# Hedgehog values: the low half taken on GpSimd from an fp32 copy instead of on VectorE from PSUM

## Chip, cores and metric

The kernel runs on one core of a Trainium2 chip. The metric is the device time of one execution in microseconds (us); less is better. The engines are named as in the profile: PE (TensorE, matmuls), DVE (VectorE), ACT (ScalarE), POOL (GpSimd, called Pool below) and SP (SyncE, which issues DMAs here). The kernel's own tiles, queues and buffers are named as in its code.

## What is computed

Four attention layers follow each other on a sequence of 2048 tokens with 512 features, each with a residual connection and a layer norm in front: softmax attention (A), Hedgehog linear attention (B), A and B again, with the same weights in both rounds. There are 32 heads of 16 features. The B layer is the one that matters here:

```python
def _B_ref(x, wqkv, w_phi, wo):
    qkv = ...                                  # x @ wqkv, split into q, k, v of 32 heads x 16
    pq = jnp.einsum("bhsd,hdf->bhsf", q, w_phi)
    pk = jnp.einsum("bhsd,hdf->bhsf", k, w_phi)
    phi_q = jnp.concatenate([_softmax(pq, axis=-1), _softmax(-pq, axis=-1)], axis=-1)
    phi_k = jnp.concatenate([_softmax(pk, axis=-1), _softmax(-pk, axis=-1)], axis=-1)
    kv = jnp.einsum("bhsf,bhsd->bhfd", phi_k, v)
    z  = jnp.einsum("bhsf->bhf", phi_k)
    num = jnp.einsum("bhqf,bhfd->bhqd", phi_q, kv)
    den = jnp.einsum("bhqf,bhf->bhq", phi_q, z)[..., None] + 1e-6
    o = num / den
    return o.transpose(...).reshape(B, S, D) @ wo

x = x + _A_ref(_layernorm(x), A_wqkv, A_wo)
x = x + _B_ref(_layernorm(x), B_wqkv, B_w_phi, B_wo)
x = x + _A_ref(_layernorm(x), A_wqkv, A_wo)
x = x + _B_ref(_layernorm(x), B_wqkv, B_w_phi, B_wo)
```

Matmuls that need more than fp16 are done with two fp16 halves: a value is rounded to fp16 (the high half), the rest that this leaves out is kept in a second fp16 (the low half), and three products (high by high, low by high, high by low) are summed. In the code these are the three `PASSES`. The values `v` of the B layer are split in this way.

## The kernel before

The two A layers take most of the time: `LayerA.attention` goes over 8 groups of heads, 4 blocks of queries and 16 tiles of keys, with scores, exp and the product with the values (lines 878 to 892). The change is in the B layers, in `LayerB.feed`, which is called four times per layer, each time for 512 tokens, and goes over four tiles of 128 tokens. I number these sixteen tiles of a layer as steps 0 to 15 (`tt` in the code); step 15 is `last` and has an order of its own.

In one step, PE projects the tile to `pk`, `pq` and `pbv` (12 matmuls each, line 1065). Each of the three is one PSUM bank of the pool `psS`, which has three buffers; one of them is held by the accumulator `kvp` for the whole layer, so that `pk`, `pq` and `pbv` take turns on two, and each waits until the one before the last has been read. Between `pq` and `pbv`, PE transposes the query features of the step before (`turn`, line 1175, the tile `pqt`), which ScalarE copies to `qT` (line 1176). After `pbv`, PE adds the key features of the step before times their values into `kvp` (`gather`, line 1182, from `fk` and `vt`). In steps 0 to 3 and 5 to 8, `between` adds work that the A layer left behind: a last output projection with its residual (`po`, `xt`, lines 586 and 574), after steps 1 and 3 the statistics of a layer norm (lines 390 to 424, the inverse root with three Newton rounds as small Pool operations), and after steps 5 to 8 the transposition of the normalised tokens into `xnTa` (lines 447, 457 on ScalarE, 460 on VectorE).

`expo` (lines 1124 to 1129) makes `f` out of `pk` or `pq`: VectorE takes maximum and minimum of each head and the two differences, ScalarE the exp. `share` (line 1144) divides by the sums: VectorE adds up (`su`, line 1135), inverts (1136) and for the keys scales by `KS` (1138), Pool multiplies `f` by it. `halves` splits the key features into `fk`: the high half on ScalarE (line 1150), the low one on Pool (1151).

The values `vt` are a tile of two fp16 halves, each with 32 rows of 16 values and a seventeenth column that Pool sets to one and to zero by memset at the beginning of a step (lines 1069 and 1070). The high half is copied from PSUM by ScalarE with a factor of 2^-8 (line 1097), the low half is computed from PSUM by VectorE (`low`, line 1092).

The order on PE, VectorE, ScalarE and Pool is that of the program here, as the feeding stage stands under `manual_schedule`: every engine takes its instructions in the order in which the code issues them, and an instruction that waits holds up all behind it on its engine. In the order of the code, a step's second half is: exp for keys, exp for queries, high half of `vt`, share of the keys, `low`, share of the queries, halves of the keys.

Of the kernel before, what the change touches and what calls it, by code (L numbers as in the profile page):

```python
# [9 lines left out]
F32 = mybir.dt.float32  # L10
# [3 lines left out]
AF = mybir.ActivationFunctionType  # L14
ALU = mybir.AluOpType
AX = mybir.AxisListType

P = 128
S = 2048
D = 512  # L20
H = 32
DH = 16
# [28 lines left out]
def mha_hedgehog_stack(ctx, tc, x_in, a_wqkv, a_wo, b_wqkv, b_wphi, b_wo, out, shmin=SHMIN):  # L51
    nc = tc.nc
# [7 lines left out]
    np_ = pool("np", bufs=2)  # L60
# [5 lines left out]
    def big(shape, dt, name):  # L66
        return bigp.tile(shape, dt, tag="big", name=name)
# [307 lines left out]
    class Norm:  # L375
# [83 lines left out]
        def low(self, t, n, ps):  # L459
            nc.vector.tensor_tensor(self.part(1, t, n), ps.rearrange("p u (c x) -> p c u x", c=NC4), self.part(0, t, n), ALU.subtract)  # L460
# [156 lines left out]
    class LayerA:  # L617
# [179 lines left out]
        def feed(self, lns, work):  # L797

            for j, (a, b, c) in enumerate(work):
                ln = lns[j]  # L800
                self.xnT.append(ln.xnT)
                ln.turn01()
                a()
                ln.turn23()
                b()
                c()
                if j == 2:
                    self.head_norms(0)
                self.head(j)
                if j == 2:  # L810
                    self.next_w = self.octet_w(1)
                    self.load_head()
                if 0 < j < NJ - 1:
                    self.head_values(j - 1)
            self.feed_end()
# [220 lines left out]
    class LayerB:  # L1036
# [15 lines left out]
        def feed(self, j, xnT, between=lambda t: None):  # L1052

            if self.kvp is None:
                self.kvp = psS.tile([P, 2, 512], F32, tag="S", name="kvp")
            qT = [big([P, 4, 512], F32, f"qT{j}_{i}") for i in range(2)]
            self.qT.append(qT)
            for t in range(4):
                tt = 4 * j + t

                def project(dst, w, passes=(0, 1, 2)):
                    for i in passes:
                        a, b = PASSES[i]
                        for c in range(NC4):
                            nc.tensor.matmul(dst, xnT[:, a, c, t * P:(t + 1) * P], w(b, c),  # L1065
                                             start=(i == 0 and c == 0), stop=(i == 2 and c == NC4 - 1))

                vt = np_.tile([P, 2, H, 17], F16, tag="yn", name="vt", bufs=5)
                nc.gpsimd.memset(vt[:, 0, :, 16:17], 1.0)
                nc.gpsimd.memset(vt[:, 1, :, 16:17], 0.0)  # L1070
                bank = lambda name: psS.tile([P, 2, 512], F32, tag="S", name=name)[:, 0, :]
                last = tt == NT - 1
                pk = bank("pk")
                project(pk, lambda b, c: self.wqk[:, 1, b, c, :])
                if last:
                    f_k = self.expo(pk)
                    self.kvb = np_.tile([P, 8, 32], F32, tag="yn", name="kvb", bufs=5)
                    nc.gpsimd.memset(self.kvb, 0.0)
                else:
                    pq = bank("pq")  # L1080
                    project(pq, lambda b, c: self.wqk[:, 0, b, c, :])
                if self.lateq is not None and tt < NT - 2:
                    self.turn(*self.lateq)
                pv_ = bank("pbv")
                project(pv_, lambda b, c: self.wv[b][:, c, :])
                if self.latek is not None:
                    self.gather(*self.latek)
                if last:
                    pq = bank("pq")
                    project(pq, lambda b, c: self.wqk[:, 0, b, c, :], (0, 1))  # L1090
                pvh = pv_.rearrange("p (h d) -> p h d", d=DH)
                low = lambda: nc.vector.scalar_tensor_tensor(
                    vt[:, 1, :, 0:16], pvh, 2.0 ** -8, vt[:, 0, :, 0:16], op0=ALU.mult, op1=ALU.subtract)
                if not last:
                    f_k = self.expo(pk)
                    f_q = self.expo(pq)
                nc.scalar.activation(vt[:, 0, :, 0:16], pvh, AF.Copy, scale=2.0 ** -8)
                if last:
                    fk = self.share_split(f_k, low)
                    self.turn(*self.todo)  # L1100
                    self.gather(tt, fk, vt)
                    project(pq, lambda b, c: self.wqk[:, 0, b, c, :], (2,))
                    self.blocks()
                    self.todo = [self.lateq, (tt, self.expo(pq), qT)]
                    for q in self.todo:
                        self.share(q[1], 1.0)
                    return
                self.share(f_k, KS)
                low()
                if tt == NT - 2:  # L1110
                    self.todo = self.lateq
                    self.latek = (tt, self.halves(f_k), vt)
                else:
                    self.share(f_q, 1.0)
                    self.latek = (tt, self.halves(f_k), vt)
                self.lateq = (tt, f_q, qT)
                between(tt)
# [290 lines left out]
```

## Time and profile before

| | us |
|---|---|
| runs: median (lowest to highest) of 3 | 2544.79 (2544.01 to 2545.54) |
| the profiled execution: its own time | 2544.9 |
| the profiled execution: span, first to last instruction | 2543.1 |
| VectorE busy in the span | 970.2 |
| ScalarE busy in the span | 2177.4 |
| Pool busy in the span | 378.4 |
| low half of `vt` on VectorE (L1092), 32 instructions | 22.0 |
| high half of `vt` on ScalarE (L1097), 32 instructions | 18.6 |
| share of `f` on Pool (L1144), 62 instructions | 119.9 |

In the rows of the profile, `out<-in` names the tile written and the tiles read, `x` a count, and the time in brackets how long the engine sat idle before the instruction and which instruction ended that. A row of the order of time begins with the start and the duration in us. A row of the groups by line has the busy time in us and the mean duration of one instruction in ns behind the bar, then the idle time before them. The rows of stretches give for each engine its busy us and its number of instructions, and then the TensorE clock that was granted. The matmuls of one projection are merged into one row.

### The profile page before, as it was taken

To read this page: it belongs to the slowest core of one execution; us is meant where nothing else is said; L and a number is where in the kernel's file an instruction comes from. 1 tells how busy PE (TensorE), PEld (TensorE's weight loads), DVE (VectorE), ACT (ScalarE), POOL (GpSimd) and SP (SyncE) were. 2 spreads that over 40 slices of the span, in tenths; PEclk is the share of its full clock that TensorE was granted. 3 is DMA by queue.
4 is the path that set the end of the run, shared out by engine and by line. 5 is a ranking of instruction groups with operands and counts; after the bars stand their busy time and mean duration, and the time that the engine had idled before them with its cause. 6 is when DMAs were issued, how large, how long until landed. Compare 5 with 4: busy or idle time off the path is not lost.

```text
span 2543.1 us, 51497 instructions
## 1 busy us (share of the span) xinstructions
PE 2436.6 (96%) x21344; PEld 748.5 (29%) x21344; DVE 970.2 (38%) x1884; ACT 2177.4 (86%) x2437; POOL 378.4 (15%) x521
## 2 busy tenths in 40 slices
PE   6799999999999999999889999999999999998998
PEld 3222222222222222345343222222222222224543
DVE  6212211212133316799871112111111111368897
ACT  5699999999999999644438999999999999994553
POOL 2100000101000000266430000000000000004552
PEclk9899999999999999999899999999999999999999
DMA  3510230033033612100234002202300251110003
GB/s 142 104 44 5 43 47 6 14 48 80 1 78 58 232 51 84 51 17 1 75 97 67 14 6 49 41 1 43 52 17 10 61 141 51 67 67 26 9 18 110
DMA packets 109782, 135.34 MB, mean 53 GB/s; under 512 B 63537, under 2 KB 64801, under 8 KB 107361
## 3 DMA queue, kind: packets, MB, share of 16 engines
q1 hardware_dynamic: 108864, 129.59, 20.6%
q8 instruction: 169, 2.77, 0.5%
q0 software_dynamic: 672, 2.36, 0.2%
q14 instruction: 77, 0.62, 0.1%
HBM read 60.06 MB, written 39.85 MB: 39 GB/s over the span
## 4 chain that ended last, share of the span: by engine, by line
PE 77%; DVE 12%; ACT 5%; issue 3%; POOL 2%; SPq 1%; DMA 0%; ACTq 0%; POOLq 0%; DVEq 0%
PE pv L892 37%; PE s L878 21%; PE pqk L586 5%; PE po L586 4%; ACT p L881 3%; DVE su L1135 2%; PE pbv L1065 1%; PE pk L1065 1%; PE pq L1065 1%; DVE f L1127 1%; POOL f L1144 1%; DVE f L1128 1%; DVE mx L1124 1%; DVE yt L531 1%; DVE su L1136 1%
## 5 line engine op out<-in xcount | busy, mean ns | idle before, releaser
L881 ACT ACTIVATE p<-s 128x1024 f32<-128x1024 f32 x2048 | 1887.9, 1114 | 21.4 <-PE s L878 18.8
L892 PE MATMUL pv<-p,v 128*32 128x512 f32 x8192 | 1092.8, 605 | 2.6 <-DVE yt L504 1.8
L878 PE MATMUL s<-kq 49*128 49x512 f16 x3872 | 605.9, 382 | 20.7 <-DMA kq<-sh 12.3
L878 PEld LDWEIGHTS <-kq 49*128 49x128 f16 x3968 | 136.3, 94 | 637.3 <-issue 625.0
L892 PEld LDWEIGHTS pv<-p,v 128*32 128x32 f32 x8192 | 161.8, 108 | 398.6 <-issue 368.5
L688 POOL TENSOR_TENSOR sq<-stg 128x512 bf16<-128x512 f16 x48 | 70.1, 1460 | 1046.1 <-DVE stg L762 943.4
L504 DVE STREAM_TRANSPOSE yt<-pv 128x512 f32<-128x512 f32 x64 | 45.8, 716 | 451.5 <-PE pv L892 429.4
L761 DVE TENSOR_SCALAR tq<-pqk,c_qk 128x512 f32<-128x512 f32 x48 | 35.9, 749 | 445.0 <-PE pqk L586 427.6
L1144 POOL TENSOR_TENSOR f<-f,su 128x1024 f32<-128x1024 f32 x62 | 119.9, 1933 | 381.0 <-DVE su L1138 351.1
L1065 PEld LDWEIGHTS <-xnTa 128*128 128x128 f16 x1152 | 110.2, 98 | 149.8 <-DVE f L1128 23.6
L586 PEld LDWEIGHTS <-wA 128*32 128x32 f16 (+1 forms) x2496 | 87.1, 98 | 202.2 <-issue 177.8
L574 DVE SCALAR_TENSOR_TENSOR xt<-po,c_oA,xt 128x512 f32<-128x512 f32 x64 | 47.1, 736 | 234.5 <-PE po L586 224.1
L586 PE MATMUL pqk<-xnTb,wA 128*32 128x512 f16 (+1 forms) x1248 | 118.5, 381 | 2.2 <-ACT xnTb L457 2.2
L586 PE MATMUL pqk<-xnT,wA 128*32 128x512 f16 (+1 forms) x1224 | 111.0, 379 | 3.1 <-ACT xnT L457 2.6
L1129 ACT ACTIVATE f<-f,c_pB 128x1024 f32<-128x1024 f32 x64 | 72.6, 1148 | 45.3 <-DVE f L1128 45.2
L1065 PE MATMUL pbv<-wbv,xnTa 128*128 128x512 f16 x384 | 91.4, 389 | 19.0 <-DVE f L1128 19.0
L1150 ACT ACTIVATE fk<-f 128x1024 f16<-128x1024 f32 x30 | 31.7, 1057 | 74.4 <-POOL f L1144 74.4
L586 PE MATMUL po<-woA,ob 128*32 128x512 f16 x1152 | 92.4, 379 | 0.0
L1065 PE MATMUL pk<-wbqk,xnTa 128*128 128x512 f16 x384 | 88.5, 379 | 0.0
L1065 PE MATMUL pq<-wbqk,xnTa 128*128 128x512 f16 x384 | 88.4, 379 | 0.0
L1135 DVE TENSOR_REDUCE su<-f 128x64 f32<-128x1024 f32 x64 | 77.5, 1211 | 9.4 <-ACT f L1129 8.8
L586 PE MATMUL po<-wbo,obB 128*128 128x512 f16 x336 | 75.9, 385 | 0.6 <-POOL obB L524 0.6
(280 smaller groups left out, 1858.8 us busy)
## 6 DMA issues: line engine op xcount, KB each, us to landing
kq<-stg SPq DMA_DIRECT2D x168, 128.0 KB
xd<-xt SPq DMA_DIRECT2D x40, 512.0 KB
xt<-xd SPq DMA_DIRECT2D x40, 512.0 KB
v<-vyt SPq DMA_DIRECT2D x384, 16.0 KB
oD<-osp SPq DMA_DIRECT2D x24, 256.0 KB
ob<-oD SPq DMA_DIRECT2D x8, 768.0 KB
xt<-in_A_x_dram SPq DMA_DIRECT2D x8, 512.0 KB
wbqk<-dBqk SPq DMA_DIRECT2D x2, 2048.0 KB
```

Source lines behind the costliest of these rows:

```text
L504: nc.vector.transpose(yt.rearrange("p a b -> p (a b)"), ps)
L574: nc.vector.scalar_tensor_tensor(xt[:, u, :], ps, co, xt[:, u, :], op0=ALU.mult, op1=ALU.add)
L586: nc.tensor.matmul(ps[r, :], w[:, r], x, start=(n == 0), stop=(n == of - 1), skip_group_check=cols)
L688: nc.gpsimd.tensor_tensor(sq, hi, hi, ALU.mult)
L761: nc.vector.tensor_scalar(tq, ps, cqk, CLAMP, op0=ALU.mult, op1=ALU.min)
L878: nc.tensor.matmul(s[:, u, :], self.side(g, half, r, 0, kt * P, P), self.side(g, half, r, 1, j * 512, 512), start=True, stop=True)
L881: nc.scalar.activation(pt, s, AF.Exp, scale=0.25 / (QS * QS))
L892: nc.tensor.matmul(acc[32 * hh:32 * hh + 32, :], self.oct[o]["v"][:, r:r + 32], pt[:, hh % 2, :], start=(kt == 0), stop=(kt == NT - 1), sk ...
L1065: nc.tensor.matmul(dst, xnT[:, a, c, t * P:(t + 1) * P], w(b, c), start=(i == 0 and c == 0), stop=(i == 2 and c == NC4 - 1))
L1129: nc.scalar.activation(f, f, AF.Exp, scale=con["pB"])
L1135: nc.vector.tensor_reduce(su, f[:, r, :], AX.X, ALU.add)
L1144: nc.gpsimd.tensor_tensor(f3, f3, self.part_sums(f3, slice(0, 64), factor), ALU.mult)
```

## The change

In steps 0 to 14, ScalarE copies `pbv` from PSUM to a new fp32 tile `vf` with the factor of 2^-8, then `vf` to the high half of `vt`; the low half is `vf` minus the high half, on Pool, in the code ahead of the share of the keys. VectorE's `low` is no longer called in these steps. In step 15 everything stays as it was. `vf` takes its buffers from the pool tag `yt`, which has three and is otherwise used in the A layers. Code above line 1097 keeps its line numbers; behind the changed lines they are three higher.

```diff
                 if not last:
                     f_k = self.expo(pk)
                     f_q = self.expo(pq)
-                nc.scalar.activation(vt[:, 0, :, 0:16], pvh, AF.Copy, scale=2.0 ** -8)
                 if last:
+                    nc.scalar.activation(vt[:, 0, :, 0:16], pvh, AF.Copy, scale=2.0 ** -8)
                     fk = self.share_split(f_k, low)
...
                     return
+                vf = np_.tile([P, H, DH], F32, tag="yt", name="vf", bufs=3)
+                nc.scalar.activation(vf, pvh, AF.Copy, scale=2.0 ** -8)
+                nc.scalar.activation(vt[:, 0, :, 0:16], vf, AF.Copy)
+                nc.gpsimd.tensor_tensor(vt[:, 1, :, 0:16], vf, vt[:, 0, :, 0:16], ALU.subtract)
                 self.share(f_k, KS)
-                low()
                 if tt == NT - 2:
```

## The prediction

> **What bounds the kernel now.** I read the page first, then busy time by stretch, then the order of time in the two kinds of step that fill the stretches, and last the groups by line for prices.
>
> ```profile
> PE 2436.6 (96%) x21344; PEld 748.5 (29%) x21344; DVE 970.2 (38%) x1884; ACT 2177.4 (86%) x2437; POOL 378.4 (15%) x521
> ...
> DVE  6212211212133316799871112111111111368897
> ```
>
> Over the span PE is busy 96% and VectorE 38%, but the slices show VectorE at 6 to 9 tenths in two places after the start: where the Hedgehog layers are fed. The change touches only these. The profiled execution took 2544.9 us around a span of 2543.1, and the median of the runs is 2544.79, so the same sum serves for both.
>
> ```profile
> 1047.30:1105.40 58.10, 51.56 (x359) 25.47 (x358) 54.76 (x88) 23.53 (x30) 32.86 (x50) 0.97 0.08 28
> 1105.40:1159.10 53.70, 49.70 (x358) 27.41 (x356) 47.43 (x75) 27.71 (x37) 31.34 (x25) 1.00 0.03 11
> 1159.10:1204.00 44.90, 44.84 (x326) 23.89 (x325) 43.38 (x69) 22.79 (x28) 29.65 (x25) 1.00 0.01 1
> ```
>
> These are the first Hedgehog layer's sixteen token tiles ("steps" 0 to 15), in three stretches (columns: length, then busy PE, weight loads, VectorE, ScalarE, Pool, each with its instructions, and PE's clock); the second layer repeats them. Steps 0 to 4: VectorE is busy 54.76 of 58.10. Steps 5 to 8: neither PE nor VectorE is full. Steps 9 to 13: PE is busy 44.84 of 44.90, so it is PE's stretch. Pool has room on average everywhere, and the average is misleading, as the next rows show. Step 7, the middle kind:
>
> ```profile
> 1132.80 1.15 ACT L1129 ACTIVATE f<-f,c_pB 128x1024 f32<-128x1024 f32 x1 [1.24 <-DVE f L1128]
> ...
> 1133.86 0.58 ACT L1097 ACTIVATE vt<-pbv 128x512 f16<-128x512 f32 x1
> ...
> 1134.52 0.20 DVE L1138 TENSOR_SCALAR su<-su 128x64 f32<-128x64 f32 x1
> 1134.63 0.69 DVE L1092 SCALAR_TENSOR_TENSOR vt<-pbv,vt 128x512 f16<-128x512 f32 x1
> 1134.86 1.93 POOL L1144 TENSOR_TENSOR f<-f,su 128x1024 f32<-128x1024 f32 x1 [4.44 <-DVE su L1138]
> ...
> 1136.83 1.06 ACT L1150 ACTIVATE fk<-f 128x1024 f16<-128x1024 f32 x1 [2.39 <-POOL f L1144]
> ...
> 1137.20 1.93 POOL L1144 TENSOR_TENSOR f<-f,su 128x1024 f32<-128x1024 f32 x1 [0.40 <-DVE su L1136]
> 1137.79 0.58 ACT L457 ACTIVATE xnTa<-pst 128x512 f16<-128x512 f32 x1
> 1138.40 0.69 DVE L460 TENSOR_TENSOR xnTa<-pst,xnTa 128x512 f16<-128x512 f32 x1 [1.38 <-ACT xnTa L457]
> ...
> 1145.97 1.93 POOL L1144 TENSOR_TENSOR f<-f,su 128x1024 f32<-128x1024 f32 x1 [4.43 <-DVE su L1138]
> ```
>
> Pool waits 4.44 us for the small scaling of `su` (L1138), then does the share of `f_k`; ScalarE's `fk` copy waits 2.39 for that; the `xnTa` copy is queued behind it on ScalarE; and VectorE's L460 waits 1.38 for that copy, with the whole next step behind it in VectorE's queue. So the start of the share of `f_k` sets the period, 1145.97 - 1134.86 = 11.11 us. VectorE's low half (L1092) lies beside the share, not in this chain.
>
> ```profile
> 1180.22 1.04 PE L1175 MATMUL pqt<-ident,f 128*128 128x128 f32 x8
> ...
> 1180.86 1.09 ACT L1176 ACTIVATE qT<-pqt 128x512 f32<-128x512 f32 x2 [2.03 <-PE pqt L1175]
> ...
> 1181.83 2.26 ACT L1129 ACTIVATE f<-f,c_pB 128x1024 f32<-128x1024 f32 x2
> ...
> 1184.00 0.58 ACT L1097 ACTIVATE vt<-pbv 128x512 f16<-128x512 f32 x1
> ...
> 1184.85 0.20 DVE L1138 TENSOR_SCALAR su<-su 128x64 f32<-128x64 f32 x1
> ...
> 1185.19 1.94 POOL L1144 TENSOR_TENSOR f<-f,su 128x1024 f32<-128x1024 f32 x1 [2.70 <-DVE su L1138]
> ...
> 1187.53 1.94 POOL L1144 TENSOR_TENSOR f<-f,su 128x1024 f32<-128x1024 f32 x1 [0.40 <-DVE su L1136]
> ...
> 1189.61 1.04 PE L1175 MATMUL pqt<-ident,f 128*128 128x128 f32 x8
> ```
>
> A step of PE's stretch: from one turn of `f_q` to the next 9.39 us (1189.61 - 1180.22). The share of `f_q` ends at 1189.47, 0.14 before the turn that needs it: PE binds, but the loop turn, ScalarE, Pool, turn is just behind.
>
> **The change, part by part.** In 30 steps (15 per layer; step 15 keeps the old way) one VectorE instruction goes, ScalarE gets a second copy, and Pool gets a subtraction that stands *ahead of* the share of `f_k` in Pool's queue. The built order shows it there, behind the memsets; PE's and SyncE's instructions keep their order, and no DMA is added or moved.
>
> ```profile
> L688 POOL TENSOR_TENSOR sq<-stg 128x512 bf16<-128x512 f16 x48 | 70.1, 1460 | 1046.1 <-DVE stg L762 943.4 <-DVE rec L506 102.7
> ...
> L1151 POOL TENSOR_TENSOR fk<-f,fk 128x1024 f16<-128x1024 f32 x30 | 63.9, 2131 | 2.3 <-ACT fk L1150 2.3
> ...
> L524 POOL TENSOR_TENSOR obB<-yb,obB 128x512 f16<-128x512 f32 x32 | 38.3, 1197 | 70.4 <-ACT obB L523 69.0 <-PE pn L1208 1.4
> ...
> L1092 DVE SCALAR_TENSOR_TENSOR vt<-pbv,vt 128x512 f16<-128x512 f32 x32 | 22.0, 686 | 0.0
> ...
> L523 ACT ACTIVATE obB<-yb 128x512 f16<-128x512 f32 x32 | 20.1, 628 | 40.7 <-DVE yb L519 40.5
> ...
> L188 POOL TENSOR_TENSOR wA_s<-wsc,wA_s 128x512 f16<-128x512 f32 x6 | 6.9, 1160 | 1.2 <-ACT wA_s L182 1.1
> ```
> ```profile
> L182 ACT ACTIVATE wA_s<-awk,sA_sc 128x512 f16<-128x512 f32 x3 | 2.1, 708 | 0.0
> ...
> L683 ACT ACTIVATE v<-pv__456 128x512 f32<-128x512 f32 x1 | 0.6, 597 | 3.1 <-PE pv__456 L679 3.1
> ```
>
> Removed: L1092, 0.686 us, of which 0.60 is engine time (the next VectorE instruction starts 0.60 after it in every full stretch). Where VectorE is full this is a gain of at most 0.60 per step; in steps 5 to 8 it only lengthens VectorE's wait for L460.
>
> Added on ScalarE: PSUM to fp32, for which L683 is the same form: 0.59 (597 ns), in the place of the old 0.58. Then fp32 to fp16 within SBUF: L523, 0.63. It reads what the copy before it wrote, so it waits for that one's end; I take 0.03. Bounds for this copy: 0.58 (L1097) and 0.71 (L182).
>
> Added on Pool: L188 is the same subtraction of 512 fp16 from fp32, 1.16; L524 has 1.20; the nearest lower bound is half of the 1024-element L1151, about 1.07, the upper one L688 with 1.46. I take 1.16, since L188 matches also in purpose, and the rows of 16 with a gap cost L1092 and L1097 nothing to be seen. Hand-overs between engines lie between 0.03 and 0.14 in the rows quoted; I take 0.06 into Pool, and 0.04 overlap of Pool instructions in sequence.
>
> [...]
>
> *The wait that is added.* Behind the subtraction on Pool's queue stand the share of `f_k`, that of `f_q`, and the low half of `fk`; for them wait ScalarE's `fk` copy, PE's turn and the gather.
>
> Steps 5 to 8. Before, the share of `f_k` starts 2.06 after the exp of `f_q` does (1134.86 - 1132.80). After: 1.06 to the first copy (1133.86 - 1132.80), +0.59 +0.03 +0.63 +0.06 +1.16 -0.04 = 3.49. Each such step is 1.43 longer. In the first of them another wait counts:
>
> ```profile
> 1105.64 1.93 POOL L1144 TENSOR_TENSOR f<-f,su 128x1024 f32<-128x1024 f32 x1 [0.38 <-DVE su L1136]
> ...
> 1107.63 1.09 PE L1175 MATMUL pqt<-ident,f 128*128 128x128 f32 x8
> ...
> 1109.29 2.19 ACT L1129 ACTIVATE f<-f,c_pB 128x1024 f32<-128x1024 f32 x2
> ...
> 1112.66 1.93 POOL L1144 TENSOR_TENSOR f<-f,su 128x1024 f32<-128x1024 f32 x1 [2.67 <-DVE su L1138]
> ```
>
> The turn in step 5 waits for the share of `f_q` (1107.57 to 1107.63), and both exps come behind its evictions on ScalarE. That share comes 1.43 late, less the 0.40 for which it now waits on its own sums: 1.03. From the exps to the share of `f_k` it is 3.37 before (1112.66 - 1109.29); after, 2.09 for the two exps less overlap, then the same copies and subtraction, 4.52: 1.15 more. So step 5 costs 2.18, and four steps 2.18 + 3 x 1.43 = 6.47.
>
> Steps 9 to 13. Entering, the turn is again 1.03 late. Then the loop closes upon itself: turn to eviction 0.64, to the exps 0.97, exps 2.09, first copy 0.59 + 0.03, second 0.63 + 0.06, subtraction 1.16 - 0.04, shares 1.89 + 1.93, hand-over to PE 0.06: 10.01, against PE's 9.39. Three such periods lie between the turns of steps 9 and 12: 3 x 0.62 = 1.86. Together 2.89.
>
> Step 14 and the end:
>
> ```profile
> 1209.06 0.89 PE L1182 MATMUL kvp<-vt,fk 128*128 128x68 f16 x23 [1.18 <-POOL fk L1151]
> ...
> 1212.77 0.20 PE L1182 MATMUL kvp<-vt,fk 128*128 128x68 f16 x1 [0.22 <-ACT fk L1165]
> ...
> 1213.63 1.20 PE L1182 MATMUL kvp<-vt,fk 128*128 128x68 f16 x23 [0.66 <-DVE fk L1166]
> ```
>
> The gather waits for Pool's low half of `fk`, now 1.43 later within its step; PE's later waits of 0.22 and 0.66 take up 0.88. Cost 0.55.
>
> Steps 0 to 4. Four step ends could each gain 0.60, -2.4. Against it: the turn of step 0 comes late as above, holding up the exps of step 1, and in steps 1 and 3 Pool's small inverse-root operations stand behind its three big ones, now later. I take 0. The lower bound is -2.4; the upper one comes from a collision:
>
> ```profile
> 1068.74 2.13 POOL L1151 TENSOR_TENSOR fk<-f,fk 128x1024 f16<-128x1024 f32 x1
> 1068.90 2.00 DVE L398 TENSOR_SCALAR ly<-lu 128x2 int32<-128x2 int32 x1
> ```
>
> L398, two elements wide, took 2.00 us: it began in Pool's `fk` and ended with it at 1070.90. After the change it arrives while the share of `f_q` still runs. If it gets in at that one's end, it is no later than now; if only after the `fk` that follows, it is 2.1 later, and in step 3 all of VectorE's next step with it: the upper bound is +2.1. [...]
>
> Sum: 0 + 6.47 + 2.89 + 0.55 = 9.9 per layer, 19.8 for two; 2544.9 + 19.8 = 2564.7 us.
>
> **Rivals.** *VectorE's relief decides* (faster). For it: 94% busy in steps 0 to 4, and Pool's average of 33 of 58 us. The gain would be 0.60 in the nine steps 0 to 8, 5.4 per layer: 2534.0. It holds if the share of `f_k` isn't moved, that is if both copies and the subtraction with their hand-overs fit into the 1.0 us (2.06 - 1.06) that `su` takes anyway; by the rows they need 2.43. At about 1.0 us less than that, a subtraction of some 0.2, the sum changes sign (ten of a layer's steps scale with it). Against it: no Pool row of this size is near 0.2. Chance 0.05.
>
> *Pool's share of the time is covered after all*, within 0.2%, which is 5 us and about what a measurement of this kernel can tell from no change: the delay per step would have to be a quarter of mine, as if Pool began with half of the second copy still to come. Nothing shows it. About 2547; chance 0.03.
>
> *Pool is dearer than its rows* (slower still): at 1.46 for the subtraction the sum rises by 10 x 0.30 = 3.0 per layer, and with L398 late by 2.1 it is 15.0, 2574.9. For it: the 2.00 above, and L688's 1.46. Against: L188 is the closer form. Chance 0.22.
>
> That the change doesn't do what it says can be left out, as the built order has the three new instructions in all 30 steps.
>
> **How the numbers follow.** My forecast has 0.70. The range goes from the low bounds (1.07 and 0.58 instead of 1.16 and 0.63: -0.14 in ten steps; steps 0 to 4 at -2.4; 6.1 per layer, 2557.1) to the dear rival with the second copy at 0.71 on top (0.08 in ten steps of two layers, 2576.5): 2556 to 2577. Slower 0.92 (forecast and dear rival), same 0.03, faster 0.05.
>
> **What would show it.** In the profile after: Pool's share of `f_k` released by Pool's own queue, no longer by L1138; its subtraction near 1.16; VectorE waiting about 3.4 us, not 1.38, for `xnTa` in steps 6 to 8 (1.43 and 0.60 more); periods of 12.5 there and of 10.0 in steps 10 to 12, with PE now idle before each turn. Wrong would be: periods of 9.4 there, a subtraction below 0.5, or a share of `f_k` that starts ahead of the subtraction.

## The result, and the profile after

The changed kernel takes 2572.05 us (median of 5 runs, 2571.09 to 2577.38), the one before 2544.79 (5 runs, 2543.59 to 2548.24): a ratio of 1.0111, 95% interval 1.01 to 1.0122. It is 27.3 us slower, where 19.8 were forecast. The execution that was profiled is the slowest of the five: 2577.38 us around a span of 2575.6. Its trace therefore shows some 5 us more than the median, and I come back to where they lie.

The page after, busy time and VectorE's slices:

```profile
PE 2449.3 (95%) x21344; PEld 752.3 (29%) x21344; DVE 962.6 (37%) x1854; ACT 2196.5 (85%) x2467; POOL 409.6 (16%) x551
...
DVE  6211211212133416878861122112121111468787
```

30 instructions have left VectorE, 30 each have come to ScalarE and Pool, and PE, with the same 21344 matmuls, is busy 12.7 us longer. PE's granted clock over the whole span is 0.980, where it was 0.983, and the short stretches below show where it drops. The three new operations, in the groups by line:

```profile
L1111 POOL TENSOR_TENSOR vt<-vf,vt 128x512 f16<-128x512 f32 x30 | 33.6, 1120 | 367.4 <-ACT vt L1110 367.4
L1110 ACT ACTIVATE vt<-vf 128x512 f16<-128x512 f32 x30 | 19.0, 633 | 0.9
L1109 ACT ACTIVATE vf<-pbv 128x512 f32<-128x512 f32 x30 | 17.7, 589 | 3.5 <-PE pbv L1065 3.5
```

1.12, 0.63 and 0.59, against 1.16, 0.63 and 0.59 in the prediction. The first layer's stretches after (columns as in the prediction; cut where steps 5 and 10 begin on VectorE and near the end of step 14, as the prediction's are, so that its second stretch also holds step 9):

```profile
1047.30:1109.90 62.60, 52.96 (x357) 25.58 (x356) 55.31 (x83) 26.49 (x34) 37.07 (x55) 0.95 0.07 26
1109.90:1170.96 61.06, 52.22 (x357) 27.52 (x356) 44.71 (x69) 31.03 (x41) 36.44 (x31) 0.97 0.03 9
1170.96:1218.50 47.54, 45.87 (x328) 23.98 (x326) 41.29 (x63) 25.78 (x33) 34.60 (x29) 1.00 0.01 2
```

In the first one PE's granted clock is 0.95 (0.97 before), in the second 0.97 (1.00 before). Only in the third is it full, and there PE, busy 44.84 of 44.90 before, now has gaps.

Steps 6 and 7 in the order of time, the chain that the prediction followed:

```profile
1131.51 3.82 POOL L1147 TENSOR_TENSOR f<-f,su 128x1024 f32<-128x1024 f32 x2
...
1140.56 1.15 ACT L1132 ACTIVATE f<-f,c_pB 128x1024 f32<-128x1024 f32 x1 [1.25 <-DVE f L1131]
1141.61 0.58 ACT L1109 ACTIVATE vf<-pbv 128x512 f32<-128x512 f32 x1
1142.22 0.63 ACT L1110 ACTIVATE vt<-vf 128x512 f16<-128x512 f32 x1
1142.27 0.20 DVE L1141 TENSOR_SCALAR su<-su 128x64 f32<-128x64 f32 x1
1142.93 1.12 POOL L1111 TENSOR_TENSOR vt<-vf,vt 128x512 f16<-128x512 f32 x1 [5.21 <-ACT vt L1110]
1144.01 3.82 POOL L1147 TENSOR_TENSOR f<-f,su 128x1024 f32<-128x1024 f32 x2
...
1147.55 0.69 DVE L460 TENSOR_TENSOR xnTa<-pst,xnTa 128x512 f16<-128x512 f32 x1 [3.37 <-ACT xnTa L457]
```

The sums `su` are ready at 1142.47, but the share of `f_k` starts at 1144.01, straight behind the subtraction: no instruction is named as its releaser any more, Pool's own queue holds it. The period is 1144.01 - 1131.51 = 12.50 (11.11 before), and VectorE waits 3.37 for `xnTa` (1.38 before). In PE's stretch:

```profile
1184.00 1.09 PE L1178 MATMUL pqt<-ident,f 128*128 128x128 f32 x8 [0.42 <-POOL f L1147]
...
1190.16 3.82 POOL L1147 TENSOR_TENSOR f<-f,su 128x1024 f32<-128x1024 f32 x2
...
1194.04 1.09 PE L1178 MATMUL pqt<-ident,f 128*128 128x128 f32 x8 [0.43 <-POOL f L1147]
```

From turn to turn 10.04 (9.39 before), with PE now idle 0.43 until Pool's shares are done (1190.16 + 3.82 = 1193.98).

What the prediction had not expected lies ahead and behind. Step 3, first before, then after:

```profile
1092.43 1.92 POOL L1144 TENSOR_TENSOR f<-f,su 128x1024 f32<-128x1024 f32 x1
1094.25 0.17 DVE L397 TENSOR_SCALAR lu<-mv 128x2 f32<-128x2 f32 x1
1094.32 2.12 POOL L1151 TENSOR_TENSOR fk<-f,fk 128x1024 f16<-128x1024 f32 x1
1094.52 1.94 DVE L398 TENSOR_SCALAR ly<-lu 128x2 int32<-128x2 int32 x1
1096.38 0.68 DVE L1124 TENSOR_REDUCE mx<-pk 128x32 f32<-128x512 f32 x1
```
```profile
1095.42 1.92 POOL L1147 TENSOR_TENSOR f<-f,su 128x1024 f32<-128x1024 f32 x1
1095.52 3.94 DVE L397 TENSOR_SCALAR lu<-mv 128x2 f32<-128x2 f32 x1
1097.31 2.12 POOL L1154 TENSOR_TENSOR fk<-f,fk 128x1024 f16<-128x1024 f32 x1
1099.57 0.17 DVE L398 TENSOR_SCALAR ly<-lu 128x2 int32<-128x2 int32 x1
1099.64 0.68 DVE L1127 TENSOR_REDUCE mx<-pk 128x32 f32<-128x512 f32 x1
```

Before, L397 came just as the share of `f_q` ended, and L398 alone was caught, in the low half of `fk`. After, L397 comes 0.10 into the share and ends with the low half of `fk` at 1099.43: two elements per partition, 3.94 us, through both Pool instructions. The next step begins 3.26 later than before (1099.64 - 1096.38). This is one of four such places in the trace. In the other three (step 1 of either layer, step 3 of the second) L397 ends with the share of `f_q`, after 1.39 to 1.44 us, and L398 is then held until the low half ends; the last section has such rows.

The end of the layer, one row of before and then the rows after, and PE's clock in two short stretches after (the last columns are the clock, DMA share and GB/s):

```profile
1209.78 1.89 PE L1065 MATMUL pq<-wbqk,xnTa 128*128 128x512 f16 x8
```
```profile
1222.76 0.20 PE L1185 MATMUL kvp<-vt,fk 128*128 128x68 f16 x1 [0.40 <-ACT fk L1153]
1224.96 1.48 PE L1185 MATMUL kvp<-vt,fk 128*128 128x68 f16 x23 [2.00 <-POOL fk L1154]
1226.25 2.91 PE L1065 MATMUL pq<-wbqk,xnTa 128*128 128x512 f16 x8
```
```profile
1102.17:1106.53 4.36, 4.36 (x18) 1.74 (x19) 4.29 (x8) 2.27 (x2) 1.31 (x8) 0.63 0.00 0
...
1224.96:1229.00 4.04, 4.04 (x32) 2.38 (x33) 3.04 (x6) 1.16 (x2) 2.87 (x5) 0.59 0.15 55
```

PE waits 2.40 in two pieces for the two halves of `fk` (1.18 before), and the 8 matmuls of `pq` behind it take 2.91 instead of 1.89, at a granted clock of 0.59. The other stretch is `pbv` in step 4: 12 matmuls, 4.36 instead of 2.75, at 0.63.

A yardstick for all that follows is how much later than before a step begins on VectorE (its first reduction of `pk`, the last row of the two fences on step 3). From such rows, in us, for both layers of the change and of the kernel of e9 below, in whose second layer no projection of PE in steps 0 to 14 is slow (that of `pq` in step 15 is):

| | steps 0 to 4 | steps 5 to 8 | steps 9 to 14 | step 15 to `pn` |
|---|---|---|---|---|
| predicted | 0 | 6.47 | 2.89 | 0.55 |
| after, layer 1 | 4.50 | 6.06 | 3.96 | 1.44 |
| after, layer 2 | 3.66 | 6.03 | 3.97 | 1.36 |
| e9, layer 2 | 2.24 | 6.64 | 2.88 | 1.52 |

### The profile page after: what moved, and what is told of

Same layout as the page of the kernel before. It is cut to its first block, busy times and chain, and to the rows that moved or that the text cites. A ratio compares the mean times of both kernels' runs of the same rounds, so it can differ in the third digit from the quotient of the medians.

```text
span 2575.6 us, 51506 instructions
## 1 busy us (share of the span) xinstructions
PE 2449.3 (95%) x21344; PEld 752.3 (29%) x21344; DVE 962.6 (37%) x1854; ACT 2196.5 (85%) x2467; POOL 409.6 (16%) x551
## 4 chain that ended last, share of the span: by engine, by line
PE 74%; DVE 8%; ACT 7%; POOL 5%; issue 4%; SPq 1%; DMA 0%; ACTq 0%; POOLq 0%; DVEq 0%
PE pv L892 37%; PE s L878 21%; PE pqk L586 5%; PE po L586 5%; ACT p L881 3%; POOL f L1147 2%; ACT f L1132 1%; PE pbv L1065 1%; POOL vt L1111 1%; PE pqt L1178 1%; DVE st L390 1%; PE pst L447 1%; DVE su L1138 1%; DVE f L1130 1%; PE pn L1211 1%
## 5 line engine op out<-in xcount | busy, mean ns | idle before, releaser
L1065 PE MATMUL pbv<-wbv,xnTa 128*128 128x512 f16 x384 | 98.8, 412 | 26.9 <-DVE f L1131 26.9
L1111 POOL TENSOR_TENSOR vt<-vf,vt 128x512 f16<-128x512 f32 x30 | 33.6, 1120 | 367.4 <-ACT vt L1110 367.4
```

What stands on the lines that cost most here:

```text
L1111: nc.gpsimd.tensor_tensor(vt[:, 1, :, 0:16], vf, vt[:, 0, :, 0:16], ALU.subtract)
```

## The experiments

**The theory**: Pool's queue. The subtraction stands ahead of the share of `f_k`, and everything behind it is late; the excess over the forecast is L397 and L398, which Pool's instructions hold up for longer than before, and PE's lower clock after some of its waits. **Rivals**: ScalarE's second copy costs it, Pool's load costs it wherever the subtraction stands, or the relief of VectorE is there and is worth little.

**e1**, the subtraction behind both shares:

```diff
-                nc.gpsimd.tensor_tensor(vt[:, 1, :, 0:16], vf, vt[:, 0, :, 0:16], ALU.subtract)
                 self.share(f_k, KS)
...
+                nc.gpsimd.tensor_tensor(vt[:, 1, :, 0:16], vf, vt[:, 0, :, 0:16], ALU.subtract)
                 self.latek = (tt, self.halves(f_k), vt)
```

> The changed kernel with one thing moved: in Pool's queue the low-half subtraction stands behind the two shares and ahead of the low half of fk, no longer ahead of the share of f_k. Same instructions on every engine. Queue theory (the loss is the share of f_k waiting behind the subtraction): the share of f_k is released by VectorE's scaling of su again, the period of steps 6 to 8 returns to 11.1 us and that of steps 10 to 12 to 9.4, VectorE's 0.60 shows in steps 0 to 4, and the total is 2539 us (2537 to 2543), faster than before by some 3 us per layer. Rival, Pool's load (30 subtractions more on Pool cost their time wherever they stand): 30 x 1.12 us remain, slower than before by 15 us or more, above 2560.

Measured: 2545.51 against 2545.16, ratio 1.0002 (0.9993 to 1.0012). Step 7 in its order of time, and step 3 of its first layer:

```profile
1138.96 3.82 POOL L1146 TENSOR_TENSOR f<-f,su 128x1024 f32<-128x1024 f32 x2 [3.79 <-DVE su L1140]
...
1142.75 1.13 POOL L1116 TENSOR_TENSOR vt<-vf,vt 128x512 f16<-128x512 f32 x1
```
```profile
1092.65 1.92 POOL L1146 TENSOR_TENSOR f<-f,su 128x1024 f32<-128x1024 f32 x1
...
1093.88 3.88 DVE L397 TENSOR_SCALAR lu<-mv 128x2 f32<-128x2 f32 x1
1094.54 1.11 POOL L1116 TENSOR_TENSOR vt<-vf,vt 128x512 f16<-128x512 f32 x1
1095.62 2.11 POOL L1153 TENSOR_TENSOR fk<-f,fk 128x1024 f16<-128x1024 f32 x1
```

The share starts again when `su` is ready, and the whole loss is gone, with all three new operations still there. So it is the place in Pool's queue; load as such is excluded. But the expected gain, 2537 to 2543, isn't there. In step 3 of the first layer, L397 sits through three Pool instructions, the end of the share of `f_q`, the subtraction and the low half, and that layer, with a slow projection in step 4 as well, is 2.9 longer than before. In the second layer L397 takes 0.29 and 0.27 and the layer is 2.7 shorter. What the executions without a trace did there isn't on record.

**e2**, no low half at all (zero by memset in steps 0 to 14) and only the old copy: the upper limit of what VectorE's relief can bring.

```diff
-                nc.gpsimd.memset(vt[:, 1, :, 16:17], 0.0)
+                nc.gpsimd.memset(vt[:, 1, :, 16:17] if tt == NT - 1 else vt[:, 1], 0.0)
...
-                nc.gpsimd.tensor_tensor(vt[:, 1, :, 0:16], vf, vt[:, 0, :, 0:16], ALU.subtract)
```

> The kernel before without VectorE's low half in steps 0 to 14: the low half of the values is left out there and set to zero by Pool's memset at the beginning of the step, so the values are those of the high half alone. It shows what VectorE's relief is worth by itself. Queue theory: only steps 0 to 4 have VectorE on the path, four to five times 0.60 per layer, 2539 to 2540 us; steps 5 to 8 keep their 11.1 and steps 10 to 12 their 9.4. Rival of the prediction (VectorE decides in steps 0 to 8): 9 x 0.60 per layer, 2534.

Measured: 2542.32 (2537.85 to 2544.57), ratio 0.9989 (0.998 to 0.9998). That is 2 above the expected 2539 to 2540. Even with no low half, and only 0.3 us more of memset on Pool per step, 2.8 us is all that is gained. The rival by which VectorE's relief decides, with 2534.0, had no room.

**e3**, both copies on ScalarE, but the low half on VectorE from PSUM as before, behind the share:

```diff
-                nc.gpsimd.tensor_tensor(vt[:, 1, :, 0:16], vf, vt[:, 0, :, 0:16], ALU.subtract)
                 self.share(f_k, KS)
+                low()
```

> Both ScalarE copies of the change (PSUM to fp32, fp32 to fp16), but the low half stays on VectorE, from PSUM, at its old place; nothing is added on Pool. Queue theory: the share of f_k is not moved, so steps 6 to 8 keep 11.1; VectorE's low half waits for the second copy and holds up the sums for f_q by 0.2 to 0.5, so steps 10 to 12 go to about 9.6 and the total rises by 3.5 to 4 us per layer, 2552 (2548 to 2556), far from the 27 us of the change. Rival (ScalarE's second copy is the cost, not Pool's subtraction): most of the 27 us, above 2560.

Measured: 2553.79 (2551.87 to 2554.77), ratio 1.0034 (1.0022 to 1.0046), as expected. The group of the low half shows how:

```profile
L1092 DVE SCALAR_TENSOR_TENSOR vt<-pbv,vt 128x512 f16<-128x512 f32 x32 | 22.2, 694 | 12.6 <-ACT vt L1110 11.5
```

VectorE now waits 12.6 us in all, nearly all of it for the second copy, and before it waited 0.0. The copies cost 8.6 where VectorE waits for them, and in e1, where nothing waits for them, they cost nothing that shows.

**e4**, the whole change, and the two statistics operations on Pool while a B layer is fed:

```diff
-            nc.vector.tensor_scalar(v, mv[:, :, 1], EPS, None, op0=ALU.add)
-            nc.vector.tensor_scalar(y.bitcast(I32), v.bitcast(I32), -0.5, 1597463007.0, op0=ALU.mult, op1=ALU.add)
+            e0 = nc.gpsimd if state.get("feedB") else nc.vector
+            e0.tensor_scalar(v, mv[:, :, 1], EPS, None, op0=ALU.add)
+            e0.tensor_scalar(y.bitcast(I32), v.bitcast(I32), -0.5, 1597463007.0, op0=ALU.mult, op1=ALU.add)
```

> The changed kernel with the two small operations L397 and L398 of the layer-norm statistics on Pool instead of VectorE, in the feeding stage only (after steps 1 and 3). Collision theory (these two, two elements wide, are shut out by Pool's running instructions, now until after the low half of fk, and hold up VectorE's whole next step): in the trace VectorE's step 4 begins 2.5 to 3 us earlier than in the changed kernel, and the total falls by 5 to 6 us to about 2566. Rival (what the prediction lacked is PE's lower clock after its longer waits alone): VectorE's step 4 begins as in the changed kernel, and the total stays at 2571 to 2574.

Measured: 2567.87 (2566.24 to 2571.06), ratio 1.0092 (1.0077 to 1.0108). In step 3:

```profile
1100.65 0.22 POOL L401 TENSOR_SCALAR lu<-mv 128x2 f32<-128x2 f32 x1
1100.96 0.19 POOL L402 TENSOR_SCALAR ly<-lu 128x2 int32<-128x2 int32 x1
```

Behind the low half of `fk` on Pool they take 0.22 and 0.19. Steps 0 to 4 come to -0.35 and -0.56 in the two layers of its trace, where the change had 4.50 and 3.66. By the distances of the medians from before (27.3 and 22.7) this is 4.6 us less, a little short of the 5 to 6 expected. It isn't yet the price of what the change adds, as the kernel before has these two operations beside Pool's as well; e5b below makes the same move there.

**e8, e6, e7**, the change in steps 0 to 4, in 5 to 8, or in 9 to 14 alone, the old way in the others:

```diff
+                if tt < 5:            # e6: 5 <= tt < 9; e7: tt >= 9
                     vf = np_.tile([P, H, DH], F32, tag="yt", name="vf", bufs=3)
...
+                else:
+                    nc.scalar.activation(vt[:, 0, :, 0:16], pvh, AF.Copy, scale=2.0 ** -8)
+                    self.share(f_k, KS)
+                    low()
```

> The change in steps 0 to 4 of each layer alone; steps 5 to 14 keep the old low half. The prediction put these steps at 0, which gives 2545. The new theory has the whole excess of the forecast here: L397 waits through two Pool instructions (about 3 us per layer), and 12 matmuls of the third projection take 4.4 instead of 2.75 us once or twice per layer after a longer wait of PE. Of the +4.5 per layer at step 5 some is PE's wait that later steps take up, so it expects +3.5 to +5 per layer: 2552 to 2555.

> The change in steps 5 to 8 of each layer alone. The prediction's term for them is 6.47 per layer, which gives 2545 + 12.9 = 2558 if the following steps take up nothing. As steps 9 and on keep the old order here, PE is the bound there again and the later turn is taken up in part: 5.4 per layer, 2556. If the whole loss sat in steps 0 to 4, this would be below 2548.

> The change in steps 9 to 14 of each layer alone. The prediction's terms for them are 2.89 and 0.55 per layer, together +6.9. The trace of the whole change has 1.5 rather than 0.55 for the end of a layer, as 8 matmuls behind PE's wait for Pool take 3 us and not 1.9; with that it is up to 4.4 per layer, +8.8. The entry of 1.03 into step 9 is counted here without the delay of steps 5 to 8, so it may be less. Expected 2549 to 2553; if the three parts of a layer simply add, what is left for this one is 2572.0 - 2544.8 - 8.6 - 14.7 = 3.9, 2548.

Measured: 2552.99 (2551.95 to 2553.85) for steps 0 to 4, 2559.03 (2558.24 to 2560.67) for 5 to 8, and 2555.95 (2553.84 to 2556.64) for 9 to 14; beside them 2544.36, 2544.36 and 2545.53 before: +8.6, +14.7 and +10.4. The first is as expected, the second 3 above the expected 2556 and 1 above what the forecast's own term gives, the third 3 above the expected range. By the starts of steps, in the layer of each trace that has fewer slow projections, the parts are 2.84, 6.41 and 4.24 (2.90 from step 9 to step 15, and 1.34 from there to `pn`), together 13.5 per layer or 27.0 for two, close to the measured 27.3. The closeness is partly chance: the 6.41 is 1.13, 1.40, 1.39 and 2.48 by steps, and the last has a slow projection in it (4.45 instead of 2.75). The medians add up to 33.7, and this is not settled: at the second `pn` the three traces stand 2.4, 0.5 and 2.0 above twice those parts (8.11, 13.29 and 10.50), in slow passages and between the layers, and why the whole change doesn't collect all of that isn't shown.

**e9**, the whole change, and unread matmuls where PE waits ahead of `pbv`:

```diff
+                for _ in range({2: 24, 4: 24, 6: 14, 7: 14, 8: 14, 9: 14}.get(tt, 0)):
+                    nc.tensor.matmul(self.kvp[:, 0, 288:512], xnT[:, 0, 0, t * P:(t + 1) * P], self.wqk[:, 0, 0, 0, 0:224],
+                                     start=False, stop=True, skip_group_check=True)
                 pv_ = bank("pbv")
```

> The whole change, and matmuls whose result nobody reads (into unused columns of the bank of kvp) ahead of the third projection in the steps where PE waits there: 24 in steps 2 and 4, 14 each in steps 6 to 9. If the 12 matmuls that take 4.4 to 5.3 us are slow because PE has waited before them, they take 2.75 again in all these steps, and the time falls by 4 to 7 us from 2572: 2565 to 2568. If the waits are no cause of it, the slow passages stay, and it stays at 2571 to 2574 or rises.

Measured: 2571.65 (2570.77 to 2573.39). Step 4 of the second layer, first in the trace of the change, then in this one:

```profile
2368.90 4.17 PE L1065 MATMUL pbv<-wbv,xnTa 128*128 128x512 f16 x12 [3.23 <-DVE f L1131]
```
```profile
2363.56 2.46 PE L1085 MATMUL kvp<-wbqk,xnTa 128*128 128x224 f16 x24
2366.91 2.76 PE L1065 MATMUL pbv<-wbv,xnTa 128*128 128x512 f16 x12 [0.89 <-DVE f L1134]
```

That the waits bring the slow passages agrees with this run; a price of theirs doesn't show. With PE busy ahead of it, `pbv` takes 2.76 instead of 4.17, and none of the steps with such matmuls is slow; the one slow `pbv` left is in step 3 of the first layer, which had none, behind a turn that waited 2.58. The span is 4.0 shorter than that of the change's profiled execution. But the median stays. So these passages seem to have lifted that one execution over its median, and as far as this run shows they are not in the 7.4 us by which the median exceeds the forecast; the traces of the other executions weren't kept.

**e10**, **e5** and **e5b**, in search of a better version: e1 with the statistics of e4 and 14 unread matmuls in steps 2 and 4; the same without those matmuls; and the kernel before with the statistics of e4 alone.

> The order of Pool's queue of the run with the subtraction behind both shares, the two small statistics operations L397 and L398 moved to Pool while a layer is fed, and 14 unread matmuls ahead of the third projection in steps 2 and 4. If the queue's order, the wait of L397 and PE's clock after waits are what held back the gain, it is 2538 to 2541, faster than before. If one of them is not, it stays at 2545 like the run with the order alone.

> The subtraction behind both shares and L397 and L398 on Pool, without any unread matmuls. If the matmuls in steps 2 and 4 did nothing in the run that had them, this is 2540 to 2541.5 as well; if PE's clock after waits is what they saved, it is 2543 to 2545.

> The kernel before (low half on VectorE from PSUM) with L397 and L398 on Pool while a layer is fed. L398 took 2.00 in steps 1 and 3 of before, half hidden: 1 to 2 per layer, 2540.5 to 2543. If it is as fast as the run with the change in the better order, the gain of that one is the statistics' and the change brings nothing in any order; if the change brings its 0.60 per step in steps 0 to 4, that one is 2 to 4 faster than this.

Measured: e10 2540.81 (2538.72 to 2541.53), ratio 0.9985 (0.9976 to 0.9994); e5 2540.49 (2537.3 to 2541.71), ratio 0.9979 (0.997 to 0.9988); e5b 2540.36 (2538.72 to 2542.05), ratio 0.998 (0.9971 to 0.9989). All three beat both kernels by what the statistics save. The unread matmuls did nothing, and the change in its better order does nothing over the kernel that never had it. Within the layers of the traces of e5 and e5b the difference is 0.2 to 0.3 us per layer (-2.04 and -1.91 against -1.71 and -1.69 from step 0 to step 15): that is what VectorE's relief is worth in that order. The order itself costs about as much with the statistics on Pool (e4 against e5: +22.7 and -5.0 from before, 27.7) as with them on VectorE (27.3 and 0.4, 26.9). And moving the statistics gains as much in the kernel before (5.2) as in the change (4.6): against e5b, e4 costs 27.9.

**e11**, the whole change, the statistics of e4, and 22 unread matmuls ahead of the gather at the end of a layer:

```diff
+                for _ in range(22 if last else 0):
+                    nc.tensor.matmul(self.kvp[:, 0, 288:512], xnT[:, 0, 0, t * P:(t + 1) * P], self.wqk[:, 0, 0, 0, 0:224],
+                                     start=False, stop=True, skip_group_check=True)
                 if self.latek is not None:
                     self.gather(*self.latek)
```

> The whole change, the two statistics operations L397 and L398 on Pool while a layer is fed, and 22 matmuls whose result nobody reads ahead of the gather of step 14 at the end of each layer, where PE waits 2.4 us in two pieces. This takes away both causes of the excess over the forecast that the traces show. If they are its causes, it is the forecast itself: 2564.7 to 2566. If PE's slower passage at the end does not come from its wait, or if it costs nothing, it is 2567 to 2569 as with the statistics moved alone.

Measured: 2564.59 (2563.42 to 2569.78), ratio 1.0076 (1.0062 to 1.0089). The end of the first layer:

```profile
1222.09 0.89 PE L1191 MATMUL kvp<-vt,fk 128*128 128x68 f16 x23 [0.47 <-POOL fk L1160]
1222.81 1.89 PE L1068 MATMUL pq<-wbqk,xnTa 128*128 128x512 f16 x8
```

The 23 and the 8 matmuls take 0.89 and 1.89 again, as before the change, and from step 15 to `pn` it is 0.28 and 0.29 in the two layers, not 1.44 and 1.36. In e4, without the 22 matmuls, that last stretch is 1.55 and 0.28, so one layer was free of the slow passage by itself. The median lies on the forecast, 2564.7, but this doesn't show the two to be the causes of the excess. The move of the statistics alone makes the kernel before 5.2 us faster, and against that kernel, e5b, the change still costs 24.2. Nor are the parts those of the forecast: in the second layer steps 0 to 4 come to -0.55 (0 predicted), step 5 to 3.03 (2.18), and step 7 has a slow projection, 1.0 more.

## Why the prediction was right, and where its sum was short

*Right in sign, mechanism and three of its terms.* The subtraction, the two copies and the hand-overs cost what their nearest rows said. Steps 5 to 8: 6.47 predicted, 6.64 in the second layer of e9, by steps 2.45, 1.39, 1.40 and 1.40 (2.18 and three times 1.43 predicted). From step 9 to step 15: 2.89 predicted, 2.88 there and 2.90 in e7; the 3.96 of the change's own trace has a slow projection in step 9. The periods of 12.5 and 10.0, the wait of 3.4 for `xnTa`, Pool's queue as the holder of the share and PE's new idle time ahead of each turn all came out. e1 shows the cause: the same operations elsewhere in the queue cost nothing that the medians can tell.

*Short: "Steps 0 to 4 ... I take 0."* It is 2.24 in the second layer of e9, just above the upper bound of 2.1, by steps -0.61, +2.07, -0.58, +1.73, -0.37. So VectorE's relief of 0.60 is there in steps 0 and 2, and is outweighed in steps 1 and 3. The step that failed is the choice between the two ends: "If it gets in at that one's end, it is no later than now". The prediction had L398 alone arrive beside the share of `f_q`. L397 stands ahead of it, and in both steps of this layer it is L397 that gets in at that end, after 1.40 us; L398 is held by the low half of `fk` once more, which ends later than before. From the start of L397 to the end of L398 it is 3.5 us there, and 2.2 before: 2.6 more per layer.

No row of before says which of the two ends it is, and no trace of the change shows the 0 that was taken: what they show in its place is 4.50, 3.66 and 2.24 (the table). In three of the four places of the change's trace L397 ends with the share of `f_q`, after 1.39 to 1.44 us, and in the fourth, with 3.94 us, it doesn't; that step costs 2.41 where the same step costs 1.73 in e9's second layer.

The collision isn't the whole of it. With the two operations on Pool in both kernels, e4 against e5b, the change costs no less, 27.9. By the starts of steps in these two traces it costs 1.3 and 1.1 per layer in steps 0 to 4, and 3.3 and 3.0 in step 5. So the 0 and the 2.18 of the forecast are too small without the collision too, and what delays these steps there wasn't followed.

*Short: "Step 14 and the end ... 0.55."* The longer wait of the gather was foreseen, and that PE's later waits take up 0.88. Not foreseen was that PE runs the matmuls behind it slower: 1.36 to 1.52 in place of 0.55, and 0.28 where it doesn't (e11, and one layer of e4). The length of a gap alone doesn't tell it here: in the change's first layer a granted clock of 0.59 follows gaps of 0.40 and 2.00, while in the second layer of e4 the 23 and the 8 matmuls behind the same two gaps take 0.89 and 1.89, as before the change. The same matmuls behind 1.18 of waiting in the kernel before, and 0.47 in e11, ran at a granted clock of 1.00.

Together, all from the second layer of e9: (2.24 - 0) + (1.52 - 0.55) + 0.17 + (-0.01) = 3.4 per layer, 6.7 for two; 2564.7 + 6.7 = 2571.4, against 2572.05 measured. The dear rival had the size of the lateness in steps 0 to 4 right and the subtraction wrong: its 1.46 was not paid, 1.12 was. That its 2574.9 lies nearer to the measurement than 2564.7 is in part luck.

*What the moved instruction cost.* On Pool the subtraction takes 1.12, 1.63 times the 0.686 of the VectorE instruction it replaced. Neither of the two places in Pool's queue made the move a gain (27.3 us slower ahead of the shares, a ratio of 1.0002 behind them), but the price that mattered wasn't the instruction's own: it was that of its place.

## What to carry to other kernels

Before moving work to an engine that is idle on average, find what stands behind it in that engine's queue: here 30 times an operation of 1.12 us with its copies in front of another cost 27 us, and behind it nothing. Ask also what the relieved engine's time is worth, by leaving the work out altogether: that run showed some 2.8 us to be had at most. And where a row of a few elements takes microseconds, look at what runs beside it: moving two operations of 128x2 off VectorE brought the only gain of this study, 5 us.

## What the runs showed of the hardware

L397, a VectorE operation on 128x2 elements that took 0.17 us in step 3 before, took 3.94 there beside two Pool instructions in sequence (after) and 3.88 beside three (e1), and ended with the last. It isn't always so. In step 1 after the change:

```profile
1068.86 1.40 DVE L397 TENSOR_SCALAR lu<-mv 128x2 f32<-128x2 f32 x1
1070.19 2.12 POOL L1154 TENSOR_TENSOR fk<-f,fk 128x1024 f16<-128x1024 f32 x1
1070.30 2.04 DVE L398 TENSOR_SCALAR ly<-lu 128x2 int32<-128x2 int32 x1
```

There L397 did end at the border between the shares and the low half (1070.26), and only L398 was held through a whole one, until 1072.34 (1070.90 before). What decides between the two wasn't tried.

PE's matmuls were slow behind some of its waits, of 1.70 (`pbv` of step 9 in the second layer after, 4.45 us) to 3.93 us (step 4 of e1, 5.30), and not behind others of the same length (1.71 in step 7 after, 2.76). Step 3 of e9 in its first and in its second layer, PE's rows:

```profile
1086.99 1.09 PE L1181 MATMUL pqt<-ident,f 128*128 128x128 f32 x8 [2.58 <-POOL f L1150]
1087.92 4.44 PE L1065 MATMUL pbv<-wbv,xnTa 128*128 128x512 f16 x12
...
2352.37 1.09 PE L1181 MATMUL pqt<-ident,f 128*128 128x128 f32 x8 [2.57 <-POOL f L1150]
2353.30 2.75 PE L1065 MATMUL pbv<-wbv,xnTa 128*128 128x512 f16 x12
```

The waits are the same to 0.01 us and the cost differs by 1.69. The granted clock of the traces tells them apart. In the traces of before and after it is 0.50 in 13 and 19 stretches and 1.00 between them, and within one trace every change of it lies a whole multiple of 3.41 us from every other; in steps 0 to 14 the stretches of 0.50 are 3.41 long, and one of them 6.83. I call the pieces of 3.41 windows. Those around each of the two waits (PE's busy time comes first behind the length):

```profile
1084.99:1088.40 3.41, 1.41 (x11) 1.17 (x12) 3.41 (x7) 1.77 (x3) 3.41 (x3) 1.00 0.00 0
1088.40:1091.81 3.41, 3.41 (x10) 1.18 (x9) 2.40 (x5) 2.44 (x3) 0.94 (x3) 0.50 0.02 5
...
2347.92:2351.34 3.42, 1.88 (x9) 0.68 (x7) 3.38 (x7) 0.88 (x1) 3.42 (x3) 1.00 0.00 0
2351.34:2354.75 3.41, 2.38 (x15) 1.60 (x16) 2.93 (x5) 1.86 (x4) 3.39 (x4) 1.00 0.00 0
```

In the first layer the wait leaves PE busy for 41% of one window, and the next window has half the clock. In the second the wait is spread over two windows, with 55 and 70%, and nothing follows. In steps 0 to 14 of both layers of before and after the clock fell so 8 times, each time behind a window in which PE was busy for 40% or less, and each such window at a clock of 1.00 had a fall behind it; two windows with 41 and 42%, both in before, had none, so that with the 41% above no single figure parts them. Of two waits of one length the dear one was here the one that lay in a single window. The profiled execution of the change lies 5.3 us above the median of its runs (2577.38 against 2572.05) with such passages in its trace, and a step's price is better read in the layer that is undisturbed.
